# Engine programs in the main part of the program instead of in a block

## The chip, the cores and the metric

The kernel runs on one core of a Trainium2 chip. A core has five engines, each with an instruction stream of its own: TensorE (PE, with its weight loads as PEld), VectorE (DVE), ScalarE (ACT), GpSimd (POOL) and SyncE (SP). They are ordered among each other by semaphores alone. Transfers between HBM and the core's SBUF run on 16 DMA engines. The metric is the device time of one execution in microseconds (us), the median of several runs.

## The reference

One decoding step for a batch of two: a layer norm, attention over the last 2048 positions of a cache (16 query heads, 8 key and value heads, head size 256), and a gate from a small dense network.

```
xn = layernorm(x)                                   # x: [2, 1, 448]
q  = (xn @ wq) -> [2, 16, 1, 256]
k, v = last 2048 rows of k_cache, v_cache           # [2, 8, 2048, 256], each used by 2 heads
p  = softmax(q k^T / 16);  s = (p v) @ wo           # wo: [4096, 448]
g  = silu(relu(xn @ w1) @ w2)                       # w1: [448, 1792], w2: [1792, 448]
out = x + s * g
```

All tensors are bfloat16.

## The kernel before, in words

All work is written down first and emitted afterwards. A small class, `_Prog` (lines 23 to 74), keeps five lists, one for each engine. `op` (line 30) appends an instruction to an engine's list with the operations that it depends on, and `dma` (line 35) appends a transfer to the list of the engine that issues it (the issue itself is line 36). The order of a list is the order of that engine's program; nothing reorders it later.

The recorded work is this. SyncE issues wq, w1 and w2, and then the keys and values of eight head pairs, 2 MB each, into three key buffers and three value buffers (`load_k` and `load_v`, lines 192 and 195). A later load waits until the buffer's previous content was used. ScalarE issues the two small loads of x (lines 180 and 182). GpSimd builds constants; VectorE makes the layer norm. TensorE computes the queries (`do_q`) and the dense network (`do_H`, `do_F`). Then a software pipeline written out by hand (the list `steps`, lines 437 to 498) runs over the eight pairs: VectorE transposes keys (`do_T`, line 346), GpSimd spreads the queries (`do_qbd`, line 297), TensorE makes the scores (`do_S`), a chain of small steps makes the softmax, and TensorE multiplies by the values (`do_PV`). Nearly all matmuls are recorded through one helper and have line 255.

The tail is in lines 529 to 557. Four transfers of wo are issued by SyncE; TensorE does 128 small matmuls with it (line 547), the last 64 of which need the last parts of wo; VectorE multiplies by the gate (line 551) and adds x (line 553); ScalarE issues the transfer of the result to HBM (line 555). The last entry of SyncE's list (line 557) is no instruction but only a wait for that transfer.

`run` (lines 40 to 74) turns the lists into programs. It gives semaphores to the operations that others depend on, and its inner `emit` goes through a list, puts the waits ahead of each operation and the increment behind it. It is called inside `with nc.Block() as block` (line 559). A block has a part for each engine: the main part of the program jumps to it (line 74, one jump per engine), the engine's list stands in it, and at its end each engine jumps to the end of the block (line 559). There every engine executes a drain and takes part in a barrier: four engines report to GpSimd, which waits for all four and then releases them.

Ahead of all this stands what the framework emits when the program object is made (line 574): GpSimd fills four constants, and a barrier of the same kind over the five engines follows.

Of the kernel before, what the change touches and what calls it, by code (L numbers as in the profile page):

```python
# [22 lines left out]
class _Prog:  # L23
# [13 lines left out]
        self.lists[eng].append(o)  # L37
        return o

    def run(self, block):  # L40
        n = 0
        for ops in self.lists.values():
            for o in ops:
                for d in o.deps:
                    d.needed = True
        for e, ops in self.lists.items():
            sem, count = self.es.enter_context(self.nc.semaphore(f"s_{e}")), 0
            for o in ops:
                if o.dma:
                    n += 1  # L50
                    o.sem, o.value = self.es.enter_context(self.nc.semaphore(f"d_{n}")), 16
                elif o.needed:
                    count += 1
                    o.sem, o.value = sem, count

        def emit(eng, ops):
            seen = {}
            for o in ops:
                want = {}
                for d in o.deps:  # L60
                    if d.value > want.get(id(d.sem), (None, 0))[1]:
                        want[id(d.sem)] = (d.sem, d.value)
                for key, (sem, value) in want.items():
                    if value > seen.get(key, 0):
                        eng.wait_ge(sem, value)
                        seen[key] = value
                made = o.fn(eng) if o.fn else None
                if o.needed:
                    made.then_inc(o.sem, 16 if o.dma else 1)

        for name, e in (("gpsimd", POOL), ("sync", SP), ("scalar", ACTE), ("vector", DVE), ("tensor", PE)):
            def body(eng, ops=self.lists[e]):
                emit(eng, ops)
            getattr(block, name)(body)


def bass_recurrent_scan__sliding_block_cached__dense_activation_relu__decode_kernel(
# [35 lines left out]
    with es:  # L113
        pr = _Prog(nc, es)
# [441 lines left out]
                     view(out_sb, 0, [[1, NCOL]], n=8, pstep=16), [v_o])  # L556
        pr.op(SP, None, [d_o])

        with nc.Block() as block:
            pr.run(block)  # L560


# [26 lines left out]
```

## Time and profile before

| what | us |
|---|---|
| median of 3 runs | 112.76 (112.56 to 113.4) |
| the profiled execution, its own time | 112.77 |
| the profiled execution, first to last instruction (span) | 110.6 |
| barrier at the start passed, first load issued | 0.73 |
| last part of wo landed | 106.08 |
| transfer of the result issued | 108.52 |

The span is shorter than the time of its execution, because the time also holds what lies ahead of the program's first instruction and behind its last one. Rows with an engine's name alone are work of that engine; a "q" behind the name (SPq, ACTq) marks what its sequencer does by itself: issuing transfers, waiting, branching, draining. Such rows are not counted as busy. "PEldq" is TensorE's sequencer where it stands beside its weight loads. A row such as "SPq L559 <- DMA out_dram<-out_sb: 19.6, 1, 19.6" says that SyncE, at an instruction of line 559, sat idle for 19.6 us in total, once, 19.6 us at the longest, until a transfer into the output landed. In the view of a line the columns are engine, operation and count, then shortest, median and longest duration in ns, then the start of the first and the last of them in us.

### The profile page before, as it was taken

The page shows a single profiled execution, that of the slowest core. Times are in us where ns is not written, and L with a number is a line of the kernel's source. Part 1 is how long each engine was busy: PE and PEld are TensorE (multiplying, and loading weights), DVE is VectorE, ACT ScalarE, POOL GpSimd, SP SyncE. Part 2 cuts the span into 40 slices and gives each one's busy share as a digit, 9 for nine tenths or more (in the row PEclk, how much of TensorE's full clock was granted, in tenths as well). Part 3 has the DMA queues.
Part 4 walks back from the last instruction along what each step waited for, and adds up shares of the span by engine and source line. Part 5 has one row for each costly group of instructions (what it writes and reads, how often), then busy time and mean ns, then how long its engine had stood idle before and what let it go on. Part 6 is the DMA issues. An engine that isn't in the chain of part 4 may idle for free.

```text
span 110.6 us, 1465 instructions
## 1 busy us (share of the span) xinstructions
PE 73.6 (67%) x594; PEld 29.8 (27%) x594; DVE 63.6 (57%) x107; ACT 18.7 (17%) x40; POOL 10.2 (9%) x48
## 2 busy tenths in 40 slices
PE   0010746778997909996980998499489987853660
PEld 0000203116332302332320332134033333331540
DVE  2164057227999658639934882995397898241001
ACT  2970000000000300212320032003202203342000
POOL 6700000500011110002020002000200000000000
PEclk9999999999999975599999589859976999999555
DMA  6798999999999999999999999999999999999930
GB/s 167 332 499 359 427 404 452 433 445 421 427 427 445 409 445 415 439 421 433 418 439 409 445 427 427 427 427 427 433 421 433 409 439 427 425 425 414 408 112 1
DMA packets 3473, 44.19 MB, mean 400 GB/s; under 512 B 394, under 2 KB 524, under 8 KB 908
## 3 DMA queue, kind: packets, MB, share of 16 engines
q1 hardware_dynamic: 3440, 44.11, 94.4%
q8 instruction: 4, 0.07, 0.2%
q10 hardware_dynamic: 28, 0.01, 0.0%
q14 instruction: 1, 0.01, 0.0%
HBM read 44.11 MB, written 0.00 MB: 399 GB/s over the span
## 4 chain that ended last, share of the span: by engine, by line
DMA 62%; PE 21%; DVE 12%; SPq 2%; issue 1%
DMA kbuf<-in_A_k_cache_dram 37%; DMA wqo<-in_A_wo_dram 15%; DMA wqo<-in_A_wq_dram 10%; DVE kt L346 7%; PE fbk L255 7%; PE sbk L255 7%; PE obk L255 5%; DVE kt L277 2%; SPq L36 2%; PE nbk L255 1%; DVE h_n L309 1%; PE mbk L255 1%; DVE rm L365 1%; DVE tmp L551 0%; DVE h_sb L318 0%
## 5 line engine op out<-in xcount | busy, mean ns | idle before, releaser
L255 PE MATMUL sbk<-kt,qbd 128*128 128x512 bf16 x128 | 39.0, 436 | 12.4 <-DVE kt L346 12.3
L346 DVE STREAM_TRANSPOSE kt<-kbuf 128x1024 f32<-128x1024 f32 x32 | 38.3, 1219 | 10.6 <-DMA kbuf<-in_A_k_cache_dram 10.6
L255 PEld LDWEIGHTS sbk<-kt,qbd 128*128 128x128 bf16 x128 | 11.5, 108 | 30.3 <-DVE kt L346 16.5
L297 POOL COPY qbd<-qall 32x32 bf16<-32x32 bf16 x32 | 6.5, 204 | 67.6 <-PE sbk L255 52.0
L255 PE MATMUL obk<-vbuf,pt 128*20 128x512 bf16 x128 | 12.1, 417 | 0.4 <-DMA vbuf<-in_A_v_cache_dram 0.4
L384 ACT ACTIVATE bias<-mbk 128x1 f32<-128x1 f32 x8 | 1.4, 170 | 42.9 <-PE mbk L255 42.9
L416 ACT ACTIVATE o_sb<-obk,rs 128x512 bf16<-128x512 f32 x8 | 5.5, 686 | 16.9 <-PE obk L255 16.9
L393 DVE STREAM_TRANSPOSE pt<-e_sb 128x512 bf16<-128x512 bf16 x8 | 5.5, 690 | 3.3 <-ACT e_sb L388 3.3
L255 PE MATMUL fbk<-w_sb,xr 128*4 128x448 bf16 x14 | 5.5, 572 | 0.7 <-DVE h_n L309 0.7
L255 PE MATMUL mbk<-ident,xg 2*128 2x2 bf16 x7 | 0.3, 164 | 8.0 <-DVE xg L225 8.0
L365 DVE TENSOR_REDUCE rm<-sbk 128x1 f32<-128x512 f32 x8 | 5.3, 662 | 0.5 <-PE sbk L255 0.5
L388 ACT ACTIVATE e_sb<-sbk,bias 128x512 bf16<-128x512 f32 x8 | 5.5, 687 | 0.3
L255 PE MATMUL obk<-wqo,xr 128*4 128x512 bf16 x28 | 3.2, 626 | 3.5 <-DMA wqo<-in_A_wq_dram 3.5
L277 DVE TENSOR_SCALAR kt<-obk 128x1024 bf16<-128x1024 f32 x2 | 2.4, 1220 | 5.3 <-PE obk L255 5.3
L255 PE MATMUL fbk<-wqo,at 128*17 128x112 bf16 x128 | 3.4, 296 | 2.9 <-DMA wqo<-in_A_wo_dram 2.9
L255 PEld LDWEIGHTS obk<-vbuf,pt 128*20 128x20 bf16 x128 | 2.9, 89 | 6.3 <-issue 4.9
L432 DVE TENSOR_TENSOR at_exp<-nbk,qmask 128x16 bf16<-128x16 f32 x16 | 1.9, 158 | 4.6 <-PE nbk L255 4.6
L375 DVE TENSOR_REDUCE mrow<-mbk 1x32 f32<-1x256 f32 x8 | 3.1, 391 | 1.5 <-PE mbk L370 1.5
L255 PEld LDWEIGHTS mbk<-one_f,mrow 1*128 1x128 f32 x16 | 2.7, 214 | 4.5 <-DVE kt L346 2.8
L551 DVE TENSOR_TENSOR tmp<-fbk,g_sb 128x112 f32<-128x112 f32 x1 | 0.3, 275 | 6.1 <-PE fbk L255 6.1
L309 DVE TENSOR_SCALAR h_n<-fbk 4x448 bf16<-4x448 f32 x2 | 1.2, 612 | 4.3 <-PE fbk L255 4.3
L255 PEld LDWEIGHTS fbk<-wqo,at 128*17 128x17 bf16 x128 | 2.8, 129 | 3.3 <-issue 1.8
(64 smaller groups left out, 49.0 us busy)
## 6 DMA issues: line engine op xcount, KB each, us to landing
kbuf<-in_A_k_cache_dram SPq DMA_DIRECT2D x8, 2048.0 KB, 21.6
vbuf<-in_A_v_cache_dram SPq DMA_DIRECT2D x8, 2048.0 KB, 18.8
wqo<-in_A_wq_dram SPq DMA_DIRECT2D x1, 3584.0 KB, 11.0
w_sb<-in_B_w_dram SPq DMA_DIRECT2D x2, 1568.0 KB, 16.0
wqo<-in_A_wo_dram SPq DMA_DIRECT2D x1, 1792.0 KB, 14.5
wqo<-in_A_wo_dram SPq DMA_DIRECT2D x1, 1232.0 KB, 16.9
wqo<-in_A_wo_dram SPq DMA_DIRECT2D x1, 448.0 KB, 17.5
wqo<-in_A_wo_dram SPq DMA_DIRECT2D x1, 112.0 KB, 17.3
```

The lines of the kernel that those rows point to most:

```text
L36: o = _Op(eng, lambda e: e.dma_start(dst, src), [d for d in deps if d is not None], True)
L255: return lambda e: e.matmul(out_ap, lhsT=lhsT, rhs=rhs, start=start, stop=stop, skip_group_check=True, **kw)
L277: v = pr.op(DVE, lambda e, par=par: e.tensor_scalar(out=view(kt[1], 128 * par, [[256, 8], [32, 4], [1, 32]]), in0=view(obk[0], par, [[64, ...
L297: st["qbd", k] = pr.op(POOL, lambda e, a=a: e.tensor_copy(view(qbd[k % 2], 16 + 32 * a, [[2, 2], [128, 8], [1, 2]], n=32, p0=32 * a), view ...
L309: st["h_n"] = pr.op(DVE, lambda e: e.tensor_scalar(out=h_n[0:4, u * (FC // 2):(u + 1) * (FC // 2)], in0=fbk[0:4, 0:FC // 2], scalar1=0.0, ...
L346: st["T", k, c] = pr.op(DVE, lambda e: e.transpose(view(dst, 32 * c, [[128, NT], [1, 32]]), view(src, 32 * c, [[128, NT], [1, 32]])), deps)
L365: st["rm", k] = pr.op(DVE, lambda e: e.tensor_reduce(out=rm[k % 2][:, :], in_=sbk[k % 2][:, :], axis=AX.X, op=ALU.max), [st["S", k], st.ge ...
L375: st["mrow", k] = st["mbk"] = pr.op(DVE, lambda e: e.tensor_reduce(out=view(mrow[k % 2], 0, [[16, 8], [1, 4]], n=1), in_=view(mbk, 0, [[0, ...
L388: st["exp", k] = pr.op(ACTE, lambda e: e.activation(e_sb[k % 2][:, :], sbk[k % 2][:, :], ACT.Exp, bias=bias[k % 2][:, 0:1], accum_out=ssum ...
L393: st["pt", k] = pr.op(DVE, lambda e: e.transpose(pt[k % 2][:, :], e_sb[k % 2][:, :]), [st["exp", k], last_PV.get(k - 2)])
L416: st["osb", k] = pr.op(ACTE, lambda e: e.activation(o_sb[k % 2][:, :], obk[k % 2][:, :], ACT.Copy, scale=rs[:, k:k + 1]), [last_PV[k], st[ ...
L432: st["at", k] = st["nbk"] = pr.op(DVE, lambda e, b=b: e.tensor_tensor(out=view(at_exp, 128 * b + 16 * k, [[4, 2], [8, 2], [1, 4]]), in0=vi ...
```

## The change

The lists are emitted into the main part of the program. There is no block any more, so no jumps to the engines' parts, no jumps to the block's end, and neither the drains nor the barrier there. The lists, their order, the semaphores and all waits inside them are the same; the barrier of line 574 at the start stays. SyncE's wait for the transfer of the result, before attached to its jump to the block's end, is now the last instruction of its program.

```diff
-    def run(self, block):
+    def run(self, nc):
         n = 0
         for ops in self.lists.values():
             for o in ops:
...
         for name, e in (("gpsimd", POOL), ("sync", SP), ("scalar", ACTE), ("vector", DVE), ("tensor", PE)):
-            def body(eng, ops=self.lists[e]):
-                emit(eng, ops)
-            getattr(block, name)(body)
+            emit(getattr(nc, name), self.lists[e])
...
         pr.op(SP, None, [d_o])
 
-        with nc.Block() as block:
-            pr.run(block)
+        pr.run(nc)
```

In the changed kernel line numbers are lower: by two from line 77 on, and by three behind line 557.

## The prediction

> **What bounds the kernel now.** I read the views from the whole to the end. First the page: busy time by engine, and the DMA row over 40 slices.
>
> ```profile
> span 110.6 us, 1465 instructions
> ...
> PE 73.6 (67%) x594; PEld 29.8 (27%) x594; DVE 63.6 (57%) x107; ACT 18.7 (17%) x40; POOL 10.2 (9%) x48
> ...
> DMA  6798999999999999999999999999999999999930
> ```
>
> No engine is busy throughout, but the DMA digit is 9 in nearly every slice until the second last: the body of the kernel is the streaming of its inputs from HBM. The chain of work that ended last says how the body meets the end.
>
> ```profile
> 0.67 0.07 issue
> 0.73 11.02 DMA wqo<-in_A_wq_dram
> ...
> 89.22 16.85 DMA wqo<-in_A_wo_dram
> 106.08 0.04 issue
> 106.12 1.75 PE fbk L255 x64
> 107.88 0.02 issue
> 107.90 0.29 DVE tmp L551
> 108.18 0.02 issue
> 108.21 0.28 DVE out_sb L553
> ```
>
> The first transfer is issued at 0.73 us, the last part of wo lands at 106.08, 64 matmuls run until 107.88, two VectorE operations until 108.49. What follows is not in the chain, because it only issues, waits and synchronizes. The timeline of the tail has the issue of the output transfer; the waits of SyncE have what it waited for; the view of line 559 has all that the block's end emits.
>
> ```profile
> 108.52 0.60 ACTq L36 DMA_DIRECT2D out_dram<-out_sb  x1
> ```
>
> ```profile
> SPq L559 <- DMA out_dram<-out_sb: 19.6, 1, 19.6
> SPq L574 <- PEq L574: 0.7, 1, 0.7
> SPq L559 <- PEq L559: 0.2, 1, 0.2
> ```
>
> ```profile
> L559 POOLq EVENT_SEMAPHORE  x2: 17/17/17, 110.4 to 110.5; - x2
> L559 POOLq DRAIN  x1: 1019/1019/1019, 77.9 to 77.9; - x1
> L559 PEldq DRAIN  x1: 422/422/422, 107.5 to 107.5; - x1
> L559 DVEq DRAIN  x1: 316/316/316, 108.2 to 108.2; - x1
> L559 ACTq DRAIN  x1: 492/492/492, 109.2 to 109.2; - x1
> L559 SPq COMPARE_BRANCH  x1: 33/33/33, 110.2 to 110.2; - x1
> L559 SPq DRAIN  x1: 13/13/13, 110.4 to 110.4; - x1
> L559 SPq EVENT_SEMAPHORE  x1: 17/17/17, 110.5 to 110.5; - x1
> L559 ACTq EVENT_SEMAPHORE  x1: 17/17/17, 110.5 to 110.5; - x1
> L559 DVEq EVENT_SEMAPHORE  x1: 21/21/21, 110.5 to 110.5; - x1
> L559 PEldq EVENT_SEMAPHORE  x1: 51/51/51, 110.5 to 110.5; - x1
> ```
>
> The tail reads so: ScalarE issues the output transfer at 108.52. SyncE waits for its landing with the jump to the block's end, which runs at 110.2. Then comes the barrier: SyncE's drain reports it as the last engine (110.4), GpSimd collects and releases (110.4 and 110.5), and the four others pass at 110.5. The last row, TensorE's of 51 ns, is the end of the span. The view's starts are rounded to 0.1 us. With its window narrowed to 110.19 to 110.20 it still holds the branch, and nothing of line 559 between 110.00 and 110.19; narrowed to 110.57 to 110.58 it holds TensorE's row alone. So the landing releases SyncE at 110.19 to 110.20, and the span ends at 110.57 to 110.58: the block's end costs 0.38 us after the landing.
>
> The profiled execution took 112.77 us, of which 110.57 are span. Thus 2.20 us lie around the span, outside of what these rows show. The median of the three runs is 112.76 (112.56 to 113.4), so the sum against the profiled execution holds for the median as well.
>
> **The change, part by part.** *The jumps at the start* (line 74, one per engine). The view of that line answers that there is nothing on it, although the jump at the end does have a row:
>
> ```profile
> nothing on L74; most used: ['L255', 'L297', 'L346', 'L65', 'L36', 'L574', 'L370', 'L388', 'L432', 'L559', 'L365', 'L375', 'L384', 'L393', 'L401', 'L416', 'L203', 'L216', 'L207', 'L211', 'L214', 'L222', 'L333', 'L225', 'L277']
> ```
>
> So a jump to what follows next anyway seems to leave no instruction. A bound from the other side: SyncE passes the start barrier, which both kernels keep, at 0.65 us (its event-semaphore row of line 574 lies in the window 0.65 to 0.66), and issues its first transfer at 0.73.
>
> ```profile
> L574 SPq EVENT_SEMAPHORE  x1: 17/17/17, 0.7 to 0.7; - x1
> ```
>
> ```profile
> 0.73 0.38 SPq L36 DMA_DIRECT2D wqo<-in_A_wq_dram  x1
> 1.17 0.42 SPq L36 DMA_DIRECT2D w_sb<-in_B_w_dram  x1
> ```
>
> From the end of the barrier row (0.65 + 0.017 = 0.67) to 0.73 are 0.06 us; from the end of the first issue (0.73 + 0.38 = 1.11) to the next (1.17) are 0.06 us too, and there is no jump between those. The jump is therefore worth 0, at most the 0.06 us of the gap. Any loss from its removal has no row. I take 0. [...]
>
> *The jump at the end.* Four of the five leave no row either; SyncE's remains because its wait for the output hangs on it. In the changed kernel that wait stands alone as the last instruction of SyncE. It is released at the same 110.19 to 110.20 and should take the 17 ns of the other event-semaphore rows in place of the branch's 33 ns. From the branch's end (110.23) to the drain (110.35: the narrowed window 110.35 to 110.36 holds it) are another 0.12 us, which go.
>
> *The drains.* GpSimd's of 1,019 ns starts at 77.9, TensorE's of 422 at 107.5, VectorE's of 316 at 108.2, ScalarE's of 492 at 109.2. The latest ends at 109.7, 0.5 us before the output lands. They cost nothing now and their removal gains nothing: SyncE's wait for the output covers them. Without that cover ScalarE's would be the last, at 109.7. SyncE's own, 13 ns, is part of the 0.38.
>
> *The barrier.* From SyncE's drain at 110.35 to the end at 110.57 are 0.22 us, which agrees with SyncE's second wait of 0.2. All of it is on the path, as nothing else runs.
>
> *What stays and what is moved.* The instructions of all five engines keep their order between the start barrier and the last one; no transfer changes its queue or place, no wait is added in the body, and behind SyncE's last wait nothing is queued. I cost the body at 0. What could move it is where the programs lie in memory, priced below.
>
> **The sum.** The span ends at SyncE's wait: 110.20 + 0.017 = 110.21. It loses 110.57 - 110.21 = 0.36 us: 0.14 of the jump and its step (0.016 + 0.12) and 0.22 of the barrier. If the 2.20 us around the span stay, the time is 112.77 - 0.36 = 112.41; against the median, 112.76 - 0.36 = 112.40. I forecast 112.4 us, 0.3% less, which is within 1% (about what a measurement of this kernel can tell from no change; the three runs spread over 0.84 us).
>
> The unknown is those 2.20 us: no row shows what is in them. Bounds from the nearest rows: nothing of them goes (then 112.4), or something of them can now start when an engine ends its own program, which for GpSimd is at 78, for VectorE at 108.5 and for ScalarE at 109.1 instead of 110.57. SyncE still ends at 110.21, so its own share stays. The other bound is that the barrier's work comes back there (0.36 us). I take nothing, which lies between. [...]
>
> **The rivals.**
>
> *More is gained behind the span.* If four engines do their ending early and only SyncE's is left, a part of the 2.20 us goes too. For it: four engines are idle at the end, GpSimd for 32 us. Against it: SyncE is the last and needs its own ending in any case. At a third of the stretch (0.73 us) the time is 111.7, at half (1.1 us) 111.3; over 1% needs 0.77 us.
>
> *It is given back.* Whatever follows has to gather the engines as well. Then the 0.36 us reappear behind the span, though the span gets shorter: 112.8. For it: the barrier's 0.22 us is the price of gathering five engines, and 2.20 us leave room for another. Against it: another gathering would stand there already and need not get longer.
>
> *The jumps cost a load of instructions.* Then the start would gain as well. The page's queues price such a load:
>
> ```profile
> q8 instruction: 4, 0.07, 0.2%
> ```
>
> 0.2% of 16 engines' 110.6 us are 3.5 us for 4 packets, 0.9 us each. Off the start, the time would be 112.4 - 0.9 = 111.5. The gap of 0.06 us at the start and the 0.12 us behind SyncE's jump at the end leave no room for one. [...]
>
> *Slower: a load of instructions becomes exposed.* The programs get shorter and may lie otherwise, so that one of the four loads of 0.9 us which now run beside other work falls where its engine has to wait for it, on the path. It decides from 0.36 us exposed. One whole load gives 112.4 + 0.9 = 113.3, two give 114.2. For it: the loads are there, in the body. Against it: what is removed at the start has no rows, and at the end little follows what is removed.
>
> **How the numbers follow.** The forecast 0.60, more behind the span 0.18, given back 0.12, a load at the jumps 0.02, slower 0.08. Of the 0.18 about 0.08 go beyond 1% (under 111.63); with the 0.02 that makes 0.10 for faster by over 1%. Half of the 0.08 exposes more than one load (over 113.89): 0.04 for slower. The rest, 0.86, is within 1%. The forecast's own range is 112.1 to 112.7, from 0.3 us to either side, the distance of the median from the lowest run (0.20) and a little more. The range of 111.6 to 112.95 holds this, the given-back case and most of the gain behind the span, and leaves out about 0.15.
>
> **What would show it.** The changed profile should have no drain, branch or GpSimd event at the end, one wait of SyncE as the last row, 0.02 us after the output lands; about 1.7 us from the issue of the output to the end of the span; a span shorter by 0.36 us if the body is the same; the first transfer still 0.06 us behind the start barrier; and instruction loads of the same count. The time less the span should stay at 2.20 us: more would be the give-back, less the gain behind the span. Wrong would be a first transfer that starts clearly closer to the barrier, a body between 0.73 and 108.5 that changes by more than 1 us, or an engine idle on "issue" in the chain where it is not now.

## The result, and the profile after

The changed kernel takes 111.61 us (median, 111.46 to 111.94), the kernel before 112.81 us in the same comparison (112.56 to 113.4). The ratio is 0.989, with a 95% interval of 0.987 to 0.992: 1.1% faster, 1.20 us. The forecast was 112.4 us, a gain of 0.36 us. So the direction held, and the gain is more than three times the forecast one.

The profiled execution of the changed kernel took 111.46 us, and its span is 110.15 us (110.2 on the page). First the page's head with its DMA row and its instruction loads, then the chain's tail, in order of time (start, duration, what):

```profile
span 110.2 us, 1454 instructions
...
DMA  6898999999999999999999999999999999999940
...
q8 instruction: 4, 0.07, 0.2%
```

```profile
88.00 18.03 DMA wqo<-in_A_wo_dram
106.03 0.04 issue
106.08 1.75 PE fbk L253 x53
107.82 0.02 issue
107.85 0.28 DVE tmp L549
108.13 0.02 issue
108.15 0.27 DVE out_sb L551
```

The issue of the result's transfer in the timeline, and the waits of SyncE:

```profile
108.46 0.59 ACTq L36 DMA_DIRECT2D out_dram<-out_sb  x1
```

```profile
SPq L65 <- DMA out_dram<-out_sb: 20.7, 1, 20.7
SPq L36 <- DVE kt L344: 11.2, 2, 5.9
SPq L571 <- PEq L571: 0.7, 1, 0.7
```

The view of line 65, where all waits that stand alone are emitted:

```profile
L65 SPq EVENT_SEMAPHORE  x1: 17/17/17, 110.1 to 110.1; - x1
```

The body is the one of before: the last part of wo lands at 106.03 (before 106.08), the result is issued at 108.46 (108.52), and there are as many instruction loads. SyncE's second wait at the end, 0.2 us in the kernel before, has gone, and its wait for the output is the last row of the program. The start has not moved. In the timeline of SyncE the first transfer still stands where it stood with the jumps:

```profile
0.73 0.36 SPq L36 DMA_DIRECT2D wqo<-in_A_wq_dram  x1
1.16 0.42 SPq L36 DMA_DIRECT2D w_sb<-in_B_w_dram  x1
```

The span is shorter by 110.57 - 110.15 = 0.42 us, 0.06 of which is the body. But the two profiled executions differ by 112.77 - 111.46 = 1.31 us. The other 0.89 us lie around the span: 2.20 us before, 1.31 after.

**What stands behind the span.** The trace holds the updates of all semaphores, also those behind the program's last instruction, which no view above shows. Semaphore 2, which the program never uses, is updated nine times there; while the last of these come and behind them, 244 others in the kernel before and 235 in the changed one are updated once each, among them those of the kernel; then semaphore 2 is updated nine times once more. Times are in us from the span's start; a time that begins with a point has the whole microseconds of the one before it, and the bar stands only to make the fifth easy to find:

```
                      span ends   first nine updates of semaphore 2                                        last of all
before                110.574     110.813 .847 111.059 .103 .127 | .224 .263 .297 111.344                  112.491
changed               110.151     107.984 109.667 .705 .749 110.272 | .316 .354 .389 110.435               111.582
```

In the kernel before, all nine come behind the span, the ninth 0.77 us after its end. In the changed kernel the first is there at 107.98, 0.19 us after TensorE's last matmul (it ends at 107.79), the second to fourth at 109.67 to 109.75, after ScalarE's last issue (it ends at 109.05, 0.62 us ahead of the second update), and only from the fifth on do they follow SyncE's wait; the ninth comes 0.28 us after the span. It looks like a gathering of the engines, one after another, and four of its steps now run ahead of the result's landing; which engine each step belongs to is tested below. From the ninth update to the last are 1.147 us in both. The second series takes 0.36 us from its first update to its ninth in both kernels. The first series takes 0.53 us in the kernel before, because its third update comes 0.21 us after the second, against 0.04 us in the second series.

### The profile page after: what moved, and what is told of

It is laid out like the page before. It is cut to its first block, busy times and chain, and to the rows that moved or that the text cites. A ratio compares the mean times of both kernels' runs of the same rounds, so it can differ in the third digit from the quotient of the medians.

```text
span 110.2 us, 1454 instructions
## 1 busy us (share of the span) xinstructions
PE 70.2 (64%) x594; PEld 28.4 (26%) x594; DVE 63.3 (57%) x107; ACT 18.7 (17%) x40; POOL 10.2 (9%) x48
## 4 chain that ended last, share of the span: by engine, by line
DMA 63%; PE 19%; DVE 14%; SPq 2%; issue 1%
DMA kbuf<-in_A_k_cache_dram 37%; DMA wqo<-in_A_wo_dram 16%; DMA wqo<-in_A_wq_dram 10%; DVE kt L344 8%; PE sbk L253 6%; PE fbk L253 6%; PE obk L253 5%; DVE kt L275 2%; SPq L36 2%; DVE h_n L307 1%; PE nbk L253 1%; DVE rm L363 1%; PE mbk L253 1%; DVE tmp L549 0%; DVE h_sb L316 0%
## 5 line engine op out<-in xcount | busy, mean ns | idle before, releaser
L253 PE MATMUL sbk<-kt,qbd 128*128 128x512 bf16 x128 | 37.8, 422 | 14.7 <-DVE kt L344 14.5
L253 PEld LDWEIGHTS sbk<-kt,qbd 128*128 128x128 bf16 x128 | 11.0, 106 | 32.1 <-DVE kt L344 20.8
L253 PE MATMUL fbk<-w_sb,xr 128*4 128x448 bf16 x14 | 4.2, 460 | 0.7 <-DVE h_n L307 0.7
L253 PE MATMUL mbk<-one_f,mrow 1*128 1x1 f32 x16 | 3.5, 288 | 0.0
```

Of the source, the lines that this page charges most:

```text
L253: return lambda e: e.matmul(out_ap, lhsT=lhsT, rhs=rhs, start=start, stop=stop, skip_group_check=True, **kw)
```

## The experiments

Theory A: the gain around the span comes from the four engines that arrive early at this gathering. Rivals: B, the jumps and the block's layout cost it; C, a barrier's own instructions cost more than their rows show. All kernels were measured in five rounds beside the kernel before, whose medians there were 112.75 to 112.80 us.

**Jumps without a barrier** (block_no_barrier). The kernel before with the end of its block emptied:

```diff
             pr.run(block)
+        nc.main_func.blocks[-1].instructions.clear()
```

> The kernel before with the instructions of the block's end removed: the jumps stay, the drains and the barrier go. Theory A (early arrival: behind the program the engines are gathered once more, one after another, and what the change gains there is that four engines go through this ahead of SyncE): all of it is kept, and only the jump of SyncE and its step come back, 0.14 us, so about 111.75 us. Theory B (the jumps and the block's layout cost the 0.9 us around the span): about as before, 112.4 to 112.8.

Measured: 111.79 us, ratio 0.990 (0.989 to 0.992). The view of the block's line has a single row, SyncE's jump:

```profile
L559 SPq COMPARE_BRANCH  x1: 33/33/33, 110.3 to 110.3; - x1
```

Of the gain of 1.20 us, 1.01 are there (112.80 - 111.79) with all jumps still in place, and the first transfer stands at 0.73 us here too. Theory B falls.

**A barrier without jumps, one and two of them** (barrier_main, barrier_twice). The changed kernel with

```diff
         pr.run(nc)
+        nc.all_engine_barrier()      # in barrier_twice: this line twice
```

> The changed kernel with one barrier over all engines at its end, in the main part, without jumps. Theory A: the barrier's own 0.22 us and the drain's step come back in the span, and behind it all engines arrive at one time again: 111.61 + 0.24 + 0.49 (the part of the difference around the span that the semaphore events show) = 112.3 us, up to 112.75 if the 0.40 us that they do not show belongs to it. Theory B: only the barrier's own price, 111.85 us.

> The changed kernel with two such barriers in a row at its end. Theory A: a second barrier has no arrival left to spoil, so it adds its own price alone, 0.2 to 0.35 us over the kernel with one. Theory C (a barrier costs about 1 us, most of it not in its rows): 0.8 to 1.1 us over the kernel with one.

Measured: 112.67 us with one (ratio 0.9987, 0.9979 to 0.9996), 113.18 with two (1.0032, 1.0018 to 1.0047). The waits of SyncE in the kernel with one barrier show its 0.2 us again:

```profile
SPq L572 <- PEq L572: 0.7, 1, 0.7
SPq L558 <- PEq L558: 0.2, 1, 0.2
```

One barrier, without any jump, brings back 1.06 of the 1.20 us; the missing 0.13 (112.80 - 112.67) is close to the 0.14 us of SyncE's jump and its step. A second one adds 0.51, less than half of the first one's 1.06, so a barrier's own price is not the main thing. That is more than the 0.2 to 0.35 expected, but short of theory C's 0.8 to 1.1. The rows of the second barrier, read in the view of its line, reach from GpSimd's drain at 110.5 to the span's end at 110.8, which is 0.3; the spans of the runs differ by 0.42 (110.88 against 110.46, means of 12), and the medians by 0.51. The semaphore events give the second barrier the price that theory A expected: from the result's landing to the ninth update of semaphore 2 are 1.06 us with one barrier and 1.38 with two, 0.32 more. Of the rest, 0.15 lie between the ninth update and the last (1.295 us against 1.144); why, no run shows.

**No barrier, but all engines late** (late_all). The changed kernel, where all five engines wait for the result's transfer as SyncE does:

```diff
-        pr.op(SP, None, [d_o])
+        for late in (SP, PE, ACTE, POOL, DVE):
+            pr.op(late, None, [d_o])
```

> The changed kernel where all five engines, not SyncE alone, wait for the transfer of the result as their last instruction: no barrier, no jump, no drain. Theory A: the span stays at 110.2 us, but the stretch behind it is the one of before: 111.61 + 0.49 = 112.1 us, up to 112.5 with the part not shown by events. Theory C (the barrier's instructions themselves): 111.6 us, as the changed kernel.

Measured: 112.35 us, ratio 0.996 (0.995 to 0.997). Line 65 shows the five waits, the last of each engine at 110.2:

```profile
L65 PEldq EVENT_SEMAPHORE  x17: 51/51/1751, 1.6 to 110.2; - x17
L65 ACTq EVENT_SEMAPHORE  x9: 17/17/17, 46.7 to 110.2; - x9
L65 DVEq EVENT_SEMAPHORE  x4: 21/21/21, 23.2 to 110.2; - x4
L65 POOLq EVENT_SEMAPHORE  x2: 17/17/17, 4.8 to 110.2; - x2
L65 SPq EVENT_SEMAPHORE  x1: 17/17/17, 110.2 to 110.2; - x1
```

There is no barrier in this kernel, its span is nearly that of the changed one (110.26 against 110.35 us, means of five and six runs), and it loses 0.74 of the 1.20 us. Lateness alone brings back 0.77 of the 0.87 us that the change saved around the span (2.10 us, against 1.33 and 2.20 in the table below): theory A holds, and theory C, which expected 111.6, falls.

**One engine late at a time** (late_pool, late_pe, late_act, late_dve). Each is the changed kernel with one line more, here for GpSimd:

```diff
         pr.op(SP, None, [d_o])
+        pr.op(POOL, None, [d_o])
```

> The changed kernel where GpSimd waits for the transfer of the result as well as SyncE; TensorE, ScalarE and VectorE still end early. Theory A1 (the gathering behind the program goes along the engines in a fixed order, and GpSimd's step is its slowest, 0.27 us ahead of it in the kernel where all wait): nearly all of the loss of the kernel where all wait, 112.1 to 112.35 us. Theory A2 (each late engine costs about the same): a fourth of that loss, 111.8 us.

> The same with TensorE in place of GpSimd. Theory A1: TensorE's step is the first of the gathering, so the chain of steps has to run from its start again, but without GpSimd's slow step: 111.61 + 0.27 = 111.9 us, up to 112.15. Theory A2: 111.8 us.

> The same with ScalarE. Theory A1: ScalarE's step is the second, between TensorE's and GpSimd's: 111.7 to 111.9 us. Theory A2: 111.8 us.

> The same with VectorE. Theory A1: VectorE's step stands next to SyncE's, so its lateness costs one step of 0.02 to 0.05 us: 111.6 to 111.7 us. Theory A2: 111.8 us.

Measured: GpSimd 112.03 us (ratio 0.994, 0.993 to 0.995), TensorE 111.96 (0.992, 0.991 to 0.993), ScalarE 111.94 (0.993, 0.992 to 0.994), VectorE 111.72 (0.991, 0.989 to 0.992). The view of line 65 of the first has GpSimd's additional wait beside SyncE's:

```profile
L65 POOLq EVENT_SEMAPHORE  x2: 17/17/17, 4.8 to 110.1; - x2
L65 SPq EVENT_SEMAPHORE  x1: 17/17/17, 110.1 to 110.1; - x1
```

By the medians alone A1's fixed order is supported, not proven: VectorE is cheapest and GpSimd dearest, as it expects, but only TensorE lies inside its numbers: VectorE and ScalarE are 0.02 and 0.04 us above theirs, GpSimd 0.07 below. TensorE, ScalarE and GpSimd are close together, and VectorE's loss of 0.11 us is not clear of the noise (its interval overlaps that of the changed kernel). The events of semaphore 2 decide. The first late one is marked with a star:

```
              span ends   first nine updates of semaphore 2
late_pe       110.226     110.416* .450 .489 .533 .556 | .654 .692 .726 110.773
late_act      110.154     107.968 110.271* .309 .354 .377 | .474 .513 .547 110.594
late_pool     110.166     107.984 109.675 110.704* .747 .770 | .868 .906 .940 110.987
late_dve      110.135     107.948 109.636 .674 110.282* .305 | .403 .441 .475 110.522
late_all      110.286     110.477* .511 .784 .828 .852 | .949 .987 111.022 111.068
```

Each lateness holds back another step: TensorE's is the first, ScalarE's the second, GpSimd's the third, VectorE's the fourth, and in the changed kernel, where SyncE alone is late, it is the fifth; four more follow. One order fits all of these five kernels and the changed one, and each step waits for the one before. GpSimd is the dear one: its step comes 0.54 us after its last instruction (110.704 against 110.166), where VectorE's and ScalarE's, behind a wait, take 0.12 to 0.15 and TensorE's 0.19. In late_pe, where the others are ready, the nine updates take 0.36 us from first to last. The losses of single engines, 0.11 to 0.42 us, add up to 1.21 us and yet all together cost 0.74: the engines get ready at the same time, so the series waits for the slowest and not for the sum. The second column of the table below shows it: with GpSimd alone late, the ninth update comes 0.86 us after the landing, just as with all five late.

**The barrier at the other end** (start_early). The framework's barrier at the start delays the first load, which goes at 0.73 us, as the block's end delayed the last step. This kernel moves SyncE's first load ahead of it:

```diff
         pr.run(nc)
+        todo = nc.main_func.blocks[0].instructions
+        first = next(i for i in todo if i.opcode == "DMACopy" and i.engine == mybir.EngineType.SP)
+        todo.remove(first)
+        todo.insert(next(n for n, i in enumerate(todo) if i.opcode == "Drain" and i.engine == mybir.EngineType.SP), first)
```

> The changed kernel with SyncE's first load (wq) moved ahead of the barrier that the framework puts at the start; everything else as it is. If the body is bound by its transfers from the first one on, the first load starts 0.66 us earlier (0.05 instead of 0.73) and the end with it: 111.61 - 0.66 = 110.95 us. Rival: the gain is lost again at the buffers' releases, since the loads behind the first eight wait for VectorE and TensorE, which are set by the norm of x and its small load, and these keep their time: 111.3 to 111.6 us.

Measured: 110.79 us, ratio 0.982 (0.981 to 0.984), 0.82 us below the changed kernel. The timeline of SyncE's first issues and two pieces of the chain:

```profile
0.00 0.37 SPq L36 DMA_DIRECT2D wqo<-in_A_wq_dram  x1
0.78 0.33 SPq L36 DMA_DIRECT2D w_sb<-in_B_w_dram  x1
```

```profile
87.28 18.14 DMA wqo<-in_A_wo_dram
105.42 0.04 issue
```

The first load goes at 0.00 instead of 0.73, and the last part of wo lands at 105.42 instead of 106.03: 0.61 us of the 0.73 come through the whole body. The rival with the buffers' releases falls. The medians differ by more than that because these two traces lie at opposite ends of their kernels' runs: the changed kernel's took 111.46 us, 0.15 below its median, and this one's 110.88, 0.09 above. Between the two profiled executions themselves the difference is 0.58 us. This is the fastest version measured.

The time less the span, as a mean over the runs of each kernel (spans rounded to 0.1 us), puts the experiments in one row. The second column is the time from the landing of the result to the ninth update of semaphore 2, from each kernel's trace:

| kernel | us around the span | us from landing to ninth update |
|---|---|---|
| start_early, changed | 1.29, 1.33 | 0.32, 0.32 |
| block_no_barrier | 1.43 | 0.43 |
| late_dve, late_pe, late_act, late_pool | 1.50, 1.64, 1.74, 1.89 | 0.44, 0.63, 0.48, 0.86 |
| late_all | 2.10 | 0.86 |
| before, barrier_main, barrier_twice | 2.20, 2.22, 2.28 | 1.16, 1.06, 1.38 |

## Why the prediction was right or wrong

The direction was right, and so was the mechanism within the span. The number was not: 112.4 was forecast and 111.61 came. That this still lies in the stated range of 111.6 to 112.95 is luck, by 0.01 us at its far end. A change within 1%, to which the text gave 0.86, did not come either; it is 1.1%.

*The jumps at the start, 0 us*: right. The first transfer stands at 0.73 in both traces, and the kernel with jumps and no barrier keeps 1.01 of the 1.20 us.

*SyncE's jump and the barrier, 0.36 us of the span*: right. From the landing of the result to the span's end the kernel before takes 110.574 - 110.180 = 0.394 us and the changed one 110.151 - 110.117 = 0.034, by the events of the transfer's semaphore: 0.36 us. The jump's 0.14 is matched by the 0.13 between barrier_main and before, and by the 0.18 between block_no_barrier and the changed kernel, as far as intervals of about 0.1 us to either side can tell.

*The drains, 0 us, covered by SyncE's wait*: right within the span. The text named their price without that cover, but not who else would like to start earlier.

*The body, 0 us*: right, 0.06 us from the issue of the first transfer to that of the result, between two single executions.

*The 2.20 us around the span, "I take nothing, which lies between"*: this is the step that failed. The stretch shrank by 0.89 us. The text had the right mechanism as a rival with a chance of 0.18: four engines do their ending early and only SyncE's is left. It priced it at a third (0.73) or a half (1.1) of the stretch, and the measured 0.89 lies between. Its main argument against it, "SyncE is the last and needs its own ending in any case", is true and was weighed too heavily: SyncE's step is the fifth of a series, and the four ahead of it are what the barrier had kept back. The trace of before had the nine updates behind the span in its semaphore events, spaced 0.53 us from first to last; the prediction rested on the views of instructions alone, where no row shows what is in the stretch. The events would have shown a gathering of about half a microsecond, and with four engines idle from 78, 107.9, 108.5 and 109.1 us on they would have spoken for the rival. That its first four steps belong to just these engines could not be read there: it took the late kernels to show it.

The working of the 1.31 us between the two profiled executions is thus: body 0.06, jump and barrier 0.36, gathering 0.77 - 0.28 = 0.49, and 0.40 that no event places. Of the last, about 0.26 goes with ScalarE: the measured time less the last event is -0.12 in the changed kernel (111.46 - 111.582) and from -0.11 to -0.13 in the kernels where ScalarE ends early, but +0.14 in late_act (111.88 - 111.740) and late_all. With a barrier it is +0.28 to +0.34, another 0.15 or so. What these two pieces are stays open: the metric's two ends are not in the trace. The 0.26 is also most of what late_all loses beyond late_pool (0.32 us of the medians), since the nine updates take equally long there.

*The giving back* fell: nothing reappeared. The gathering that it supposed is there, as the nine updates of semaphore 2, but its ninth comes 0.28 us after the changed span, against 0.77 us before. *A load of instructions at the jumps* fell with theory B. *Slower through exposed loads* fell: the count and the body stayed.

## What to carry to other kernels

What follows the last instruction of a program belongs to the time as well (0.89 us of the 1.31 between the profiled executions lay around the span), and if it goes through the engines one after another, as the late kernels show it here, each engine should be let go as soon as it has nothing to do. A barrier of one's own at the end holds all of them back to the last one: here its rows showed 0.22 us, and it cost 1.06. Let only one engine wait for the last transfer, choose the one whose turn comes last (here SyncE, the fifth), and read the semaphore events behind the span, not its instructions alone; and where the first load needs nothing from the start-up, issue it ahead of the barrier there (0.82 us of the medians here).

## What the runs showed that was not expected

One order of the engines behind the program fits the changed kernel and the five late ones: TensorE, ScalarE, GpSimd, VectorE, SyncE; a step took 0.02 to 0.10 us where its engine was ready. GpSimd needed 0.54 us from its last instruction to its step in late_pool, and being late cost most there: 0.42 us of the medians. The jumps to a part that follows anyway left no row in the trace, while the one jump that carried a wait cost about 0.14 us with its step. Moving a single issue ahead of the start barrier was worth 0.82 us of the medians in a kernel of 111.61.
